# Another order of the same operations in a two-layer linear-attention and MLP kernel

## The chip, the cores and the metric

The kernel runs on one core of a Trainium2 chip. A time is the device time of one execution in microseconds (us); what counts is the median of several executions. The engines of a core run side by side and meet at semaphores: TensorE (PE in the profile, its weight loads PEld) multiplies matrices, VectorE (DVE), ScalarE (ACT) and GpSimd (POOL) work element by element, SyncE (SP) issues the DMA transfers. Each engine takes its instructions in the order in which the program gives them.

## The reference

Two layers of attention without softmax, each followed by an MLP with GELU, on `x` of 2048 rows and 448 columns. The same weights serve both layers.

```python
def _A_ref(x, wqkv, wo):
    ...
    phi = lambda t: jnp.where(t > 0, t + 1, jnp.exp(t)) + 1e-6
    pq, pk = phi(q), phi(k)
    kv = jnp.einsum("bhsd,bhse->bhde", pk, v)
    z = jnp.einsum("bhsd->bhd", pk)
    num = jnp.einsum("bhqd,bhde->bhqe", pq, kv)
    den = jnp.einsum("bhqd,bhd->bhq", pq, z)[..., None] + 1e-6
    o = num / den
    return (lambda x, *d: x.transpose(*d))(o, 0, 2, 1, 3).reshape(B, S, D) @ wo

def _B_ref(x, w1, b1, w2, b2):
    h = jnp.einsum("bsd,df->bsf", x, w1) + b1
    h = _gelu(h)
    return jnp.einsum("bsf,fd->bsd", h, w2) + b2

x = x + _A_ref(_layernorm(x, axis=-1), A_wqkv, A_wo)
x = x + _B_ref(_layernorm(x, axis=-1), B_w1, B_b1, B_w2, B_b2)
x = x + _A_ref(_layernorm(x, axis=-1), A_wqkv, A_wo)
x = x + _B_ref(_layernorm(x, axis=-1), B_w1, B_b1, B_w2, B_b2)
```

There are 16 heads of 28 columns; the MLP is 1792 wide.

## The kernel before, in words

**Number format.** A 32-bit operand goes through TensorE as a high and a low part (`hi`, `lo`), both in the format fp32r. A product of two such operands is made of three: hi by hi, hi by lo, lo by hi. ACT makes the high part by a copy, DVE or GpSimd the low part by a subtraction. The 448 columns are three pieces of 128 and a tail of 64; the tails of both parts share one piece, so a full product is 3 x 3 + 2 = 11 matmuls.

**Tiles.** The 2048 rows are 16 tiles of 128, and four blocks of four tiles. The MLP's 1792 inner columns are 14 chunks of 128; with four blocks this gives 56 chunks to a layer, counted through: chunk n belongs to block n // 14.

**Operations.** Each short function with `@op` gives one operation for a layer, a tile or chunk number and perhaps an engine. Those that matter here:

- Attention, first half, for each tile t: `ld` loads the rows, `a`, `ar`, `n` normalize them (statistics on DVE, a root on GpSimd, the norm on DVE). `T` turns the tile by four transposes on TensorE (with `d`, the tail's copy), or `tu` on DVE with `st` and `sp` through DRAM; `xh`, `xl` make its two parts. `K` and `Q` are products with the weights (lines 543 to 548), `ke`, `kp`, `kh`, `kl`, `za` and `qe`, `qp`, `qs` what follows on ACT, DVE and SP. `sh`, `sl` split the tile as it is, and `G` (lines 617 to 621) adds its product with K to four banks that stay for all 16 tiles.
- Attention, middle: `z`, `zb`, `dc`, `gt`, `kv`, `mask`, `m`, `mh`, `ml`, `mc` make the small matrices from G.
- Attention, second half, for each tile: `pl` loads the kept Q, `pz` (GpSimd), `pd`, `pm` (DVE) divide; `pT` (four transposes on TensorE) or `pu`, `ps`, `pp` turn it; `qh`, `ql` split it; `o` or `oc` are the products, `oa` adds to x; `la`, `ar`, `ln` normalize for the MLP, `mT` (TensorE) or `mu`, `ms`, `mp` turn, `yh`, `yl` split; `lb` adds the second bias on GpSimd.
- MLP, for each chunk: `f` is the first product, 11 matmuls of 512 columns (lines 850 to 854). `g` is the GELU on ACT (line 859), `gh` its high part on ACT, `gl` its low part on DVE (line 869). `y` is the second product, four groups `u` of three matmuls of 448 columns (lines 877 to 879), added up over the 14 chunks of a block in four banks. `ya` adds to x, `ys` stores.

**Buffers.** The PSUM banks are four for sums (`acc`), two for `f`, `Q` and `T` (`h`) and two others (`m`). The results of `g` have three buffers (ring `e`), and the rings `A` and `B` hold `gh` and `gl` of two chunks. A buffer is taken again when its last reader is done, which is a wait of the writer's engine.

**Order.** The whole schedule is written out by hand in `ORDER` (lines 15 to 110): two strings of tokens, one for each layer. `run` (lines 904 to 909) takes the tokens one by one and calls the operation; `>` in front of a token means the next layer, `<` the layer before, and an engine may follow a colon. So the text fixes the order of the instructions on each engine and on each DMA queue, and nothing else; the waits follow from which tile is written and read.

```python
    def run(l, text):
        for tok in text.split():
            up = (tok[0] == ">") - (tok[0] == "<")
            tok, _, e = tok.lstrip("<>").partition(":")
            name = tok.rstrip("0123456789")
            ops[name.replace("_", "")](l + up, int(tok[len(name):] or 0), e)
```

Of the kernel before, what the change touches and what calls it, by code (L numbers as in the profile page):

```python
# [16 lines left out]
        "ld0 a0 ar0 ld1 a1 n0 hot16 wkld0 wkld1:a wkld2 wkld3:a wkh1 wkl1 ht0 wkh0 ar1 wkl0 n1 d0 ht1 hx0 hl0 hk0 "  # L17
        "wkh2 wkl2 wkh3 d1 ht3 hx1 hl1 wqld0 wqh0 ht2 hx2 wkl3:p hk1 hx3 hl2 hk2 hl3 wql0 hk3 ld2 wqld1 wqh1 a2 "
        "ke0 kp0 bld1:xn wqld2 wqh2 wqld3 wqh3 kh0 sh0 wql2 wql3 wql1:p Q0 ar2 n2 d2 T2 sh1 sl0 kl0 G0 ld3 ld7 a3 "
        "za0 qe0 qp0 xh2 xl2 ke1 ld4 ld9 a4 kp1 kh1 ld6 bld0:xn sl1 ar4 n4 za1 ar3 ld5 n3 d3 a5 qs0 bhi0 ar5 blo0 "  # L20
        "Q1 qe1 K2 tab0 ke2 bld2:xn ld8 kl1 G1 T3 a7 qp1 n5 ar7 bhi1 blo1 kp2 a6 xh3 xl3 sh3 sh2 sl2 d4 kh2 Q2 T4 "
        "K3 n7 kl2 G2 ar6 qe2 bhi2 blo2 sl3 xh4 n6 za2 a8 qp2 tu6 tu7 ar8 bld3:xn ld10 qs1 bias1 xl4 a10 sh4 sl4 "
        "ar10 bld4:xn ke3 d5 bhi3 blo3 Q3 qs2 st3 ld11 ld12 bld5:xn kp3 n8 za3 n10 qe3 qp3 a11 kh3 bhi4 kl3 K4 "
        "ke4 kp4 Q4 kh4 T5 xh5 sp3 blo4 bhi5 blo5 ar11 fl kl4 qs3 xl5 tu10 n11 a9 za4 tu8 G3 G4 bld6:xn bld7:xn "
        "bias2 ld14 sh6 xh6 sl6 xl6 qe4 sh5 xh7 ar9 n9 ld13 tu9 st4 K5 bhi6 blo6 qp4 ke5 kp5 tu11 za5 sl5 bhi7 "
        "blo7 Q5 qe5 kh5 bld9:xn bhi9 qs4 a12 sp4 K6 ke6 qp5 qs5 xl7 kl5 kp6 kh6 za6 kl6 Q6 G5 K7 ar12 blo9 n12 "
        "bld8:xn st5 bld11:xn qe6 a14 xh8 bhi8 blo8 bld10:xn xh9 ke7 tu12 xl9 bhi11 sh7 a13 qp6 kp7 xl8 sp5 blo11 "
        "sl7 ar14 ar13 bhi10 kh7 kl7 n14 blo10 Q7 G6 qe7 sh8 qp7 K8 ld15 a15 n13 ke8 kp8 za7 G7 Q9 qs6 bld12:xn "
        "bhi12 sl8 blo12 ar15 qs7 bld13:xn tu14 kh8 tu13 xh10 sh9 za8 kl8 xl10 bhi13 blo13 K9 ke9 kp9 bld14:xn "
        "st6 bhi14 blo14 sl9 K10 ke10 kh9 Q8 qe8 bld15:xn bhi15 xh11 bld16:xn wo1 n15 kp10 za9 kl9 tu15 G8 G9 "  # L30
        "blo15 sh10 sl10 xl11 K11 sh11 sl11 kh10 kl10 bhi16 blo16 qp8 za10 G10 sp6 xh12 st7 xl12 K12 bld17:xn "
        "bld18:xn ke11 xh13 kp11 xl13 za11 qe9 kh11 bhi17 kl11 G11 ke12 kp12 za12 sh13 blo17 sl13 sh12 kh12 sl12 "
        "bhi18 sp7 xh15 K13 Q10 kl12 blo18 G12 xh14 xl14 K14 ke13 kp13 kh13 za13 kl13 xl15 K15 bld19:xn qs8 wo0 "
        "sh14 bld21:xn wv1 ld1 wv0 pl1 bhi19 qe10 blo19 ke14 bhi21 blo21 kp14 sl14 qp9 kh14 kl14 qp10 G13 G14 "
        "ke15 kp15 za14 za15 ld2 ld3 bld20:xn bld22:xn pl3 ld5 sh15 kh15 sl15 z zb pz1 kl15 G15 gt0 bhi20 Q11 dc "
        "pd1 gt3 gt1 gt2 kv pm1 pT1 Q12 pz3 pd3 pl2 pl0 blo20 pz0 mask pd0 m3 pm0 pz2 qs9 bld23:xn ld0 pd2 pm3 "
        "qh1 ql1 pT0 qh0 ql0 m0 mh0 ml0 m1 mh1 ml1 m2 mh2 ml2 mh3 ml3 pT3 qe11 pl4 pl7 bld24:W6 o0 pm2 ld6 pT2 "
        "oa0 qp11 qs11 qh2 bhi23 blo23 la0 o1 ql2 o2 oa1 ar0 ln0 lx0 mT0 bhi24 qh3 bhi22 la1 ql3 o3 oa2 yh0 ar1 "
        "blo22 la2 ln1 yl0 lx1 Q13 mT1 pz4 ar2 qe12 oa3 qp12 ln2 lx2 mT2 Q14 la3 ar3 yh1 yl1 ln3 qe13 qp13 lx3 "
        "bld25:W5 qs10 yh2 pd4 yl2 qe14 qp14 qs12 mT3 yh3 yl3 bhi25 blo25 pl5 pz5 Q15 qe15 qp15 qs14 qs15 qs13 "  # L40
        "blo24 f0 g0 gh0 pm4 lb1 pu4 pd5 pm5 gl0 f4 g4 f1 g1 gh1 u0 pl6 pz6 pd6 u3 u2 u1 f6 f2 g2 gl1 y1 bld27:W5 "
        "pu5 g6 gh2 gl2 f7 f3 g3 pm6 ps2 pp2 mc bld26:W6 pl8 pz7 pd7 gh3 y2 gl3 y3 f5 bhi26 qh5 gh4 pu6 ql5 oc5 "
        "pm7 gl4 ld4 y4 g5 qh4 gh5 bhi27 blo27 blo26 ql4 oc4 gl5 pu7 ps3 gh6 bld29:W5 ld7 bhi29 bld28:W6 ld8 pp3 "
        "pl9 f9 y5 g9 gh9 oa5 gl6 oa4 la4 y6 ar4 pz8 blo29 pd8 g7 qh6 qh7 f10 ln4 la5 gl9 mu4 ql7 ar5 pm8 ln5 gh7 "
        "gl7 mu5 g10 oc7 oa7 f11 g11 f8 g8 y7 f12 lb3 ql6 ms2 mp2 pl10 oc6 la7 ar7 gh8 gl8 y8 g12 ln7 oa6 la6 pz9 "
        "ar6 ln6 gh11 y9 lb2 bhi28 gh10 lb7 pd9 mu6 gl10 mu7 ms3 yh4 yh5 f13 mp3 pl11 y10 gh12 pm9 gl11 yl4 y11 "
        "g13 lb0 gl12 gh13 gl13 blo28 y12 yl5 y13 pz10 yh6 yh7 yl6 yl7 pu8 pd10 pu9 f14 g14 gh14 ya3 pm10 ya0 ya1 "
        "pl13 ys0 ys1 gl14 pu10 pz11 ya2 pd11 ps4 ys2 pp4 pl12 ys3 ld9 ld13 f15 g15 gh15 qh8 pm11 pu11 gl15 ql8 "
        "u58 u59 ld11 ps5 u56 f16 f17 u57 y15 g17 qh9 oc8 oa8 g16 pz12 tab1 gh16 gl16 f18 y16 la8 gh17 ql9 pd12 "
        "oc9 f20 pp5 pl15 qh10 g18 ql10 oc10 ar8 lb6 oa9 gl17 gh18 gl18 y17 ld10 g20 qh11 ln8 ql11 oc11 la9 lb8 "  # L50
        "ar9 pz13 ln9 gh20 oa11 pm12 mu8 f21 f19 la11 mu9 gl20 y18 g19 g21 pd13 f24 oa10 la10 pm13 gh19 gl19 y19 "
        "f22 y20 ar10 lb4 ar11 lb5 lb9 pl14 ln11 ln10 pz14 gh21 gl21 y21 lb11 g22 pd14 mu10 ms4 mp4 yh8 g24 gh22 "
        "gl22 gh24 yh9 mu11 pm14 ms5 f23 g23 y22 yl9 yl8 pu12 pu13 gh23 gl23 f27 g27 f25 mp5 yh10 yh11 yl11 g25 "
        "y23 yl10 pu14 gl24 f26 g26 gh25 gl25 f28 f30 y24 y25 gh26 gl26 y26 ps6 g28 g30 gh27 gl27 pz15 pd15 y27 "
        "ya7 ya5 ya4 >wkld0 pp6 ys7 ys5 gh28 gl28 f29 g29 qh13 u115 u112 u113 f34 pm15 ql13 pu15 gh29 gl29 oc13 "
        "oa13 ya6 f32 g32 u114 y29 qh12 gh30 gh32 la13 gl32 gl30 f31 g31 ps7 pp7 ld12 ld14 y30 g34 gh31 lb10 ql12 "
        "oc12 qh15 f35 oa12 gl31 y31 la12 ar12 ln12 lb12 mu12 ql15 qh14 ql14 g35 ar13 y32 f33 g33 gh33 >wqld0 "
        "oc14 oa14 gl33 ln13 la14 ar14 mu13 gh34 gl34 f37 f39 y33 ms6 ys6 ld15 mp6 >wqld1 ys4 >ld0 gh35 g37 >wkh1 "
        "g39 gl35 oc15 oa15 la15 ln14 mu14 ar15 ln15 mu15 ms7 lb15 y34 f38 f36 g36 gh36 y35 gh37 yh12 gl36 y36 "
        "gl37 y37 g38 gh38 gl38 y38 f40 gh39 gl39 mp7 yl12 yh15 yl15 >a0 yh14 yl14 lb13 f41 g41 yh13 yl13 g40 "  # L60
        "gh40 y39 f42 gh41 g42 gl40 y40 f43 f44 gh42 gl41 y41 g44 >wqh1 gh44 >wql1:p ya11 g43 ya8 ya9 >wkld1 ys8 "
        "ya10 gl42 f46 f45 g46 ys9 gl44 u169 u170 u168 u171 g45 gh43 gl43 ys10 >ld4 ys11 >ld2 >a2 >ar0 >n0 "
        ">wkl1:p f47 y43 y44 gh45 gl45 >wkh2 gh46 gl46 >wqh3 >wql3 y45 >ar2 >n2 >tu0 >ld1 >ld3 >a3 >a1 >ar1 >ar3 "
        "g47 gh47 >n1 >wqh2 f48 y46 >wkh3 g48 f50 >tu1 >a4 gl47 y47 gh48 >st0 g50 gh50 gl48 y48 f51 >wqh0 g51 "
        ">wql2 >ar4 >n4 gl50 f49 g49 f53 f52 gh49 gl49 y49 >wkl3 g52 gh51 >n3 >tu2 >wkl2 gl51 g53 f54 f55 y50 y51 "
        ">wkh0 gh52 gl52 y52 >wkl0 >tu3 >wql0 >sp0 >xh0 gh53 g55 g54 gl53 y53 gh54 >st1 gl54 y54 >sh0 >sl0 >xl0 "
        ">K0 gh55 gl55 y55 >tu4 >xh1 >xl1 ya13 ya12 >ld5 >sp1 lb14 ya14 ys13 ys12 >ld6 ya15 ys15 "
    ),
    (
        "ke0 Q0 K1 Q1 xh2 xh3 kp0 kh0 ke1 xl2 a5 ar5 xl3 n5 za0 tu5 qe0 <ys14 ld7 kl0 G0 a6 sh1 qe1 qp1 ld8 st2 "  # L70
        "sp2 sl1 kp1 kh1 kl1 a7 ar7 qp0 wo1 ld10 ar6 n6 za1 K2 ke2 kp2 kh2 kl2 za2 Q2 qe2 qp2 n7 tu6 ld9 qs1 qs2 "
        "xh4 sh3 xh5 xl4 a9 ar9 a8 n9 tu7 a10 ar8 Q3 G1 K3 ke3 n8 kp3 qe3 qp3 st3 sh2 sl3 sl2 kh3 Q4 K4 ke4 kl3 "
        "za3 xl5 kp4 G2 K5 G3 sh5 kh4 za4 ld12 ld11 ar10 sl5 tu8 tu9 n10 a12 tu10 kl4 sp3 qs0 xh6 xl6 Q5 ke5 sh4 "
        "qe4 kp5 kh5 a11 K6 ar12 sl4 G4 ke6 qp4 ar11 n11 tu11 xh7 st4 sp4 qs4 Q6 kl5 n12 xl7 kp6 qe5 qp5 sh6 sl6 "
        "kh6 ld13 a13 za5 qs3 st5 sp5 G5 K7 kl6 G6 ar13 tab0 sh7 qe6 xh8 tu12 n13 tu13 xl8 qp6 za6 ld14 qs5 ld15 "
        "a15 ke7 kp7 kh7 kl7 K8 ke8 Q7 a14 xh9 xl9 xh11 xl11 sh8 sl7 G7 ar15 za7 kp8 n15 qe7 qp7 kh8 sh9 K9 st6 "
        "sp6 xh12 kl8 ke9 kp9 za8 sl8 ar14 G8 n14 tu14 xh10 xl10 Q9 za9 sh10 sl10 xh13 kh9 kl9 tu15 st7 K10 ke10 "
# [863 lines left out]
```

## Time and profile before

| what | value |
|---|---|
| runs | 880.39 us median of three (880.34 to 881.69) |
| span of the profiled execution | 878.3 us |
| HBM read and written | 55.65 and 34.08 MB, 102 GB/s over the span |
| first attention stage, first MLP stage | about 20 to 140 us, 140 to 443 us |
| second attention stage, second MLP stage | about 443 to 575 us, 575 to 873 us |

The profile is a record of one execution. The span goes from its first to its last instruction; the run's time is some 2 us longer. "Busy" is the time in which an engine has an instruction in hand. Matmuls overlap on TensorE, so the duration of one (0.36 us for 448 columns) is longer than the distance between the starts of two (0.20 us), and it is the distance that adds up. In a timeline the columns are start, duration, engine, line, operation, written tile and read tiles, sizes, and how many were merged; in brackets the engine's idle time before it and what ended that. In a list of waits they are the waiting engine and line, what it waited for, then the total, the number and the longest in us.

### The profile page before, as it was taken

To read this page: it belongs to the slowest core of one execution; us is meant where nothing else is said; L and a number is where in the kernel's file an instruction comes from. 1 tells how busy PE (TensorE), PEld (TensorE's weight loads), DVE (VectorE), ACT (ScalarE), POOL (GpSimd) and SP (SyncE) were. 2 spreads that over 40 slices of the span, in tenths; PEclk is the share of its full clock that TensorE was granted. 3 is DMA by queue.
4 is the path that set the end of the run, shared out by engine and by line. 5 is a ranking of instruction groups with operands and counts; after the bars stand their busy time and mean duration, and the time that the engine had idled before them with its cause. 6 is when DMAs were issued, how large, how long until landed. Compare 5 with 4: busy or idle time off the path is not lost.

```text
span 878.3 us, 11548 instructions
## 1 busy us (share of the span) xinstructions
PE 873.2 (99%) x4181; PEld 772.4 (88%) x4181; DVE 473.7 (54%) x972; ACT 336.4 (38%) x596; POOL 202.6 (23%) x239
## 2 busy tenths in 40 slices
PE   9999999999999999999999999999999999999998
PEld 7999988889888888888899998988888888888887
DVE  7886587356574343324378765954572743343112
ACT  6777634332223221424355653333233132223221
POOL 4665543123132011010023333130220220130000
PEclk9999999999999999999999999999999999999999
DMA  6675732541613023221065452233125142120101
GB/s 210 175 234 171 222 95 98 159 130 58 213 58 117 30 82 103 78 84 49 24 206 160 138 182 85 94 124 99 65 88 166 46 119 84 39 96 5 38 1 43
DMA packets 62763, 93.71 MB, mean 107 GB/s; under 512 B 8817, under 2 KB 57969, under 8 KB 62705
## 3 DMA queue, kind: packets, MB, share of 16 engines
q1 hardware_dynamic: 62400, 92.51, 34.2%
q8 instruction: 33, 0.54, 0.3%
q10 hardware_dynamic: 304, 0.46, 0.2%
q14 instruction: 26, 0.20, 0.1%
HBM read 55.65 MB, written 34.08 MB: 102 GB/s over the span
## 4 chain that ended last, share of the span: by engine, by line
PE 99%; DVE 0%; ACT 0%; issue 0%; POOL 0%; POOLq 0%
PE y L878 10%; PE y L879 10%; PE y L877 10%; PE hp L851 9%; PE hp L852 9%; PE hp L850 9%; PE hp L854 3%; PE hp L853 3%; PE G L618 2%; PE psq L543 2%; PE G L617 2%; PE G L619 2%; PE psq L545 2%; PE psq L544 2%; PE psk L543 2%; PE psk L545 2%
## 5 line engine op out<-in xcount | busy, mean ns | idle before, releaser
L869 DVE TENSOR_TENSOR gl<-g,gh 128x512 fp32r<-128x512 f32 x112 | 79.8, 720 | 193.1 <-ACT gh L211 192.7
L878 PE MATMUL y<-w2l,gh 128*128 128x448 f32 x448 | 163.7, 365 | 0.0
L877 PE MATMUL y<-w2h,gh 128*128 128x448 f32 x448 | 163.6, 365 | 0.0
L879 PE MATMUL y<-w2h,gl 128*128 128x448 f32 x448 | 163.6, 365 | 0.0
L859 ACT ACTIVATE g<-hp,b1s 128x512 f32<-128x512 f32 x112 | 76.3, 688 | 227.8 <-PE hp L854 208.5
L851 PE MATMUL hp<-XH,w1l 128*128 128x512 f32 x336 | 131.2, 391 | 0.0
L852 PE MATMUL hp<-XL,w1h 128*128 128x512 f32 x336 | 131.1, 390 | 0.0
L850 PE MATMUL hp<-XH,w1h 128*128 128x512 f32 x336 | 131.1, 390 | 0.0
L211 ACT CAST gh<-g 128x512 fp32r<-128x512 f32 x112 | 69.1, 620 | 154.9 <-PE y L878 143.3
L357 POOL TENSOR_TENSOR brs<-bve,mhalf 128x1 f32<-128x1 f32 x64 | 41.0, 642 | 318.7 <-DVE bve L351 317.6
L877 PEld LDWEIGHTS y<-w2h,gh 128*128 128x128 f32 x448 | 84.1, 188 | 8.3
L878 PEld LDWEIGHTS y<-w2l,gh 128*128 128x128 f32 x448 | 84.1, 188 | 7.9
L879 PEld LDWEIGHTS y<-w2h,gl 128*128 128x128 f32 x448 | 84.1, 188 | 6.6
L852 PEld LDWEIGHTS hp<-XL,w1h 128*128 128x128 f32 x336 | 63.1, 188 | 13.6
L851 PEld LDWEIGHTS hp<-XH,w1l 128*128 128x128 f32 x336 | 63.1, 188 | 11.9
L850 PEld LDWEIGHTS hp<-XH,w1h 128*128 128x128 f32 x336 | 63.1, 188 | 11.8
L716 POOL TENSOR_TENSOR pz<-pq,zb 128x448 f32<-128x448 f32 x32 | 37.7, 1181 | 70.2 <-DVE dn L721 43.8
L535 POOL TENSOR_TENSOR xnl<-x,xnh 128x384 fp32r<-128x384 f32 x32 | 33.9, 1058 | 81.6 <-ACT xnh L211 81.2
L428 DVE TENSOR_TENSOR XL<-sp,XH 128x512 fp32r<-128x512 f32 x50 | 36.9, 752 | 22.7 <-ACT XH L211 22.5
L795 DVE TENSOR_TENSOR x<-op,x 128x448 f32<-128x448 f32 x32 | 19.8, 618 | 48.0 <-PE op L789 47.2
L853 PE MATMUL hp<-XH,w1x 128*128 128x512 f32 x112 | 43.6, 389 | 0.0
L854 PE MATMUL hp<-XL,w1x 128*128 128x512 f32 x112 | 43.6, 389 | 0.0
(162 smaller groups left out, 1573.1 us busy)
## 6 DMA issues: line engine op xcount, KB each, us to landing
x<-in_A_x_dram SPq DMA_DIRECT2D x32, 224.0 KB, 4.0
pq_d<-eq SPq DMA_DIRECT2D x32, 224.0 KB, 2.7
pq<-pq_d SPq DMA_DIRECT2D x32, 224.0 KB, 3.2
x<-x_d SPq DMA_DIRECT2D x32, 224.0 KB, 3.7
sq_a<-sq SPq DMA_DIRECT2D x13, 512.0 KB, 3.0
sp<-sq_a SPq DMA_DIRECT2D x52, 128.0 KB, 3.1
sq_q<-sq SPq DMA_DIRECT2D x12, 512.0 KB, 3.0
sp<-sq_q SPq DMA_DIRECT2D x48, 128.0 KB, 3.3
```

Source lines behind the costliest of these rows:

```text
L211: act.copy(out, src)
L357: pool.tensor_tensor(rs, ve, mhalf, op=OP.pow)
L850: pe.matmul(o, w1h[:, c, s], x.moving(x.hi, c), start=(c == 0), stop=False)
L851: pe.matmul(o, w1l[:, c, s], x.moving(x.hi, c), start=False, stop=False)
L852: pe.matmul(o, w1h[:, c, s], x.moving(x.lo, c), start=False, stop=False)
L853: pe.matmul(o, w1x[:, s], x.moving(x.hi, 3), start=False, stop=False)
L854: pe.matmul(o, w1x[:, s], x.moving(x.lo, 3), start=False, stop=True)
L859: act.activation(T[l, "g", n], T[l, "hp", n], AF.Gelu_apprx_tanh, bias=b1s[:, n % NF:n % NF + 1])
L869: dve.tensor_sub(lo, T[l, "g", n], f(hi))
L877: pe.matmul(o, gh[:, r], w2h[:, i, s], start=first, stop=False)
L878: pe.matmul(o, gh[:, r], w2l[:, i, s], start=False, stop=False)
L879: pe.matmul(o, gl[:, r], w2h[:, i, s], start=False, stop=last)
```

## The change

Only the text in `ORDER` is new; no operation, engine, buffer or tile size is. Both texts hold the same 2,122 operations, and the tokens that issue transfers (`ld`, `bld`, `qs`, `pl`, `st`, `sp`, `ps`, `pp`, `ms`, `mp`, `ys` and so on) come in the same sequence. The text is the same up to `d2`. Behind it, tokens have changed places: in the MLP the `f` of several chunks follow on each other and then the `y` of several; `T`, `pT` and `mT` of two tiles stand side by side; operations of ACT, DVE and GpSimd stand at other places between. The cut between the first and the second string has moved, too: operations that stood as `>wkl0` at the end of the first now stand at the start of the second, where `<gh51` is the first layer's.

```diff
-        "ke0 kp0 bld1:xn wqld2 wqh2 wqld3 wqh3 kh0 sh0 wql2 wql3 wql1:p Q0 ar2 n2 d2 T2 sh1 sl0 kl0 G0 ld3 ld7 a3 "
-        "za0 qe0 qp0 xh2 xl2 ke1 ld4 ld9 a4 kp1 kh1 ld6 bld0:xn sl1 ar4 n4 za1 ar3 ld5 n3 d3 a5 qs0 bhi0 ar5 blo0 "
-        "Q1 qe1 K2 tab0 ke2 bld2:xn ld8 kl1 G1 T3 a7 qp1 n5 ar7 bhi1 blo1 kp2 a6 xh3 xl3 sh3 sh2 sl2 d4 kh2 Q2 T4 "
...
+        "wqh1 a2 ke0 kp0 bld1:xn wqld2 wqh2 wqld3 wqh3 kh0 sh0 wql2 wql3 wql1:p Q0 ar2 n2 d2 ld3 ld7 ld4 ld9 "
+        "ld6 bld0:xn T2 za0 bhi1 qe0 kl0 sh1 sl0 G0 sl1 ke1 a3 qp0 ar3 a4 kp1 n3 xh2 ar4 xl2 n4 sh3 bhi0 blo0 "
+        "ld5 qs0 a5 bld2:xn ld8 Q1 qe1 a6 ar5 n5 qp1 kh1 K2 d3 za1 kl1 ke2 Q2 a7 T3 kp2 ar7 za2 xh3 kh2 xl3 ar6 "
+        "qe2 kl2 d5 d4 G1 K3 blo1 fl T4 n7 sh2 qp2 tu7 ke3 sl2 xh4 a8 T5 n6 ar8 kp3 G2 bld3:xn ld10 sl3 xl4 "
...
-        "yl1 la3 ar3 ln3 lx3 qe13 qp13 yh2 qs13 yl2 Q14 qe14 qp14 mT3 yh3 yl3 Q15 pd4 qe15 qs14 pl6 f0 g0 gh0 "
-        "qp15 qs15 gl0 pz5 pd5 pm5 pm4 pu4 f1 g1 gh1 pz6 pd6 lb2 lb3 pu5 pm6 gl1 u3 u0 u1 f2 g2 f4 g4 f5 u2 f3 g3 "
-        "y1 gh2 gl2 f6 y2 g5 ps2 mc pp2 qh4 gh3 pu6 ql4 gl3 f7 g7 gh5 qh5 lb1 pz7 pd7 ql5 oc4 f8 y3 pm7 pu7 ps3 "
...
+        "wkl0 <gh51 wqh2 <gl51 wqh0 <y50 ar3 n0 wkl1:p tu0 n3 a2 wql2 <y51 <f53 ar2 a1 ar1 n1 tu1 st0 sp0 <g53 "
+        "wqh3 <gh53 <f54 n2 <gl53 <g54 tu3 <f52 wql3 <f55 wkh3 <g52 <gh52 <gl52 xh0 <y52 <g55 xl0 <gh54 <gl54 "
+        "tu4 <y53 wkl2 xh1 wkl3 tu2 sh0 sl0 <y54 <gh55 K0 <gl55 wql1:p xl1 <y55 <ya13 ke0 K1 wql0 <ya12 <ya15 "
+        "kp0 <ya14 Q0 za0 kh0 st1 sh1 ld5 sp1 xh2 kl0 xh3 <ys13 <ys12 ld6 <ys15 <ys14 ld7 ld8 a5 ar5 qe0 n5 tu5 "
...
+        "f0 g0 gh0 pz6 f1 g1 f2 lb2 gh1 gl1 f3 gl0 u1 g3 u2 pd6 pz7 pd7 u0 u3 y1 pm7 g2 gh2 pm6 pu6 mc pu7 pp2 "
+        "ps3 pl9 pl8 pp3 gl2 y2 gh3 gl3 y3 tab1 f5 g5 f4 qh4 g4 gh4 pz9 f7 qh5 ql4 pd9 gl4 f6 g6 pz8 gh5 pd8 "
...
+        "gl16 oc10 y15 y16 pz15 oa8 pm13 la8 gh17 gl17 gh18 gl18 y17 y18 qh11 oc9 oa9 la9 f22 pd15 ar8 ln8 mu8 "
+        "oa10 g22 f20 f19 g20 gh20 ar9 ln9 lb9 pm15 la10 f21 gl20 ql11 g19 oc11 gh19 gl19 y19 y20 ar10 g21 gh21 "
+        "gh22 ln10 mu9 gl21 pm12 pu15 mu10 pu12 y21 gl22 y22 ms4 ys0 ld11 oa11 la11 f23 g23 f24 pu13 lb7 ar11 "
...
```

164 rows, old and new, of the table ORDER are left out of this document.

## The prediction

> **What bounds the kernel now.** I read the page first, then busy time by stretch, then the waits of the matrix engine alone, then single stretches of the timeline.
>
> ```profile
> span 878.3 us, 11548 instructions
> PE 873.2 (99%) x4181; PEld 772.4 (88%) x4181; DVE 473.7 (54%) x972; ACT 336.4 (38%) x596; POOL 202.6 (23%) x239
> ```
>
> ```profile
> 20.00:140.00 120.00, 120.00 (x615) 107.99 (x614) 94.49 (x197) 75.86 (x148) 61.91 (x75) 1.00 0.56 168
> 140.00:443.00 303.00, 303.00 (x1421) 266.48 (x1420) 141.00 (x284) 94.40 (x158) 54.11 (x54) 1.00 0.30 93
> 443.00:575.00 132.00, 131.97 (x668) 118.80 (x667) 98.06 (x209) 70.39 (x129) 37.17 (x51) 1.00 0.47 146
> 575.00:873.00 298.00, 298.00 (x1397) 262.10 (x1396) 123.75 (x245) 82.27 (x136) 40.21 (x38) 1.00 0.23 69
> ```
>
> ```profile
> PE hot L228 <- POOL ones L170: 1.1, 1, 1.1
> PE psk L489 <- ACT XH L211: 0.2, 1, 0.2
> PE tp L465 <- ACT tail L211: 0.2, 1, 0.2
> ```
>
> The columns of the stretches are PE, PEld, DVE, ACT and POOL. The column behind POOL is the granted clock, 1.00 throughout. From 20 to 873 us TensorE is as good as never seen idle, and its whole list of waits is 1.5 us long, all of it in the launch. So the time is the list of its 4,181 products at their spacing. A new order of the same products can win in three ways only: closer spacing, a shorter launch, a shorter end. The launch (up to the token d2) and the order of the last tokens (y54, y55, the ya and ys of the last four tiles) stay. That leaves the spacing. It can lose more: each product that now comes before its data adds its wait to the end one for one.
>
> **The change part by part.** Counted token by token, both orders hold the same 2,122 operations; the sequence of all tokens that issue a DMA is the same one, so each SP queue entry keeps its neighbours and only the time at which its data is ready can shift. No wait is added by hand; waits follow from the order.
>
> *First products in runs.* I took the TensorE tokens out of both texts. In the old order the 112 `f` stand in 72 runs (40 of one, 25 of two, 6 of three, 1 of four); in the new one in 25 (1 of two, 2 of three, 10 of four, 8 of five, 4 of six, so longer than the short description says). What a run's start costs is seen in the one run of four:
>
> ```profile
> 410.93 0.39 PE L850 MATMUL hp<-XH,w1h 128*128 128x512 f32 x1
> ...
> 413.45 0.39 PE L850 MATMUL hp<-XH,w1h 128*128 128x512 f32 x1
> ...
> 420.93 0.36 PE L877 MATMUL y<-w2h,gh 128*128 128x448 f32 x1
> ```
>
> ```profile
> 276.15 0.39 PE L850 MATMUL hp<-XH,w1h 128*128 128x512 f32 x1
> ...
> 278.66 0.39 PE L850 MATMUL hp<-XH,w1h 128*128 128x512 f32 x1
> ...
> 281.15 0.36 PE L877 MATMUL y<-w2h,gh 128*128 128x448 f32 x1
> ```
>
> The rows are starts of `f` operations (eleven products each). After a second product (`y`) the first takes 413.45 - 410.93 = 2.52 us, the three behind it (420.93 - 413.45) / 3 = 2.49 each; in the run of two, which also follows a `y`, 2.51 and 2.49. So a run costs 0.01 to 0.03 us to open, and I take 0.02. The new order opens 72 - 25 = 47 fewer: 47 x 0.02 = **0.94 us less**, with ends at 0.47 and 1.41. [...]
>
> *Transposes side by side.* Six more groups of four now follow directly on another group (T4 T5; pT1 pT3, mT1 mT0, mT2 mT3 in the first layer, where mT1 mT2 were adjacent before; pT2 pT3, mT0 mT1, mT3 mT2 in the second). One such pair and one single group are in the trace:
>
> ```profile
> 128.67 0.60 PE L390 MATMUL tp<-ident,xm 128*128 128x128 f32 x4
> 129.02 0.45 PE L774 MATMUL op<-Mh,qh 112*128 112x448 f32 x1
> 129.31 0.36 PE L775 MATMUL op<-Ml,qh 112*128 112x448 f32 x1
> ```
>
> ```profile
> 133.78 1.06 PE L390 MATMUL tp<-ident,xm 128*128 128x128 f32 x8
> 134.60 0.45 PE L543 MATMUL psq<-wq,XH 128*128 128x448 f32 x1
> 134.89 0.37 PE L544 MATMUL psq<-wq,XH 128*128 128x448 f32 x1
> ```
>
> Four transposes and the slow first product behind them take 129.31 - 128.67 = 0.64 us; a usual product of 448 columns is 0.20, so the group costs 0.44. Eight take 134.89 - 133.78 - 0.20 = 0.91, against twice 0.44 = 0.88. A pair is 0.03 dearer, not cheaper: 6 x 0.03 = **0.18 us more**. Its ends are nothing and 0.36, since the starts are rounded to 0.01. A gain I exclude: the first slow product is saved once per pair, and the 0.91 already contains that.
>
> *Spacing of the attention products.* The 448-column products of K, Q and G go at two paces, whatever their line:
>
> ```profile
> 60.78 0.37 PE L617 MATMUL G<-kh,xnh 128*128 128x448 f32 x1
> ...
> 62.84 0.37 PE L621 MATMUL G<-kl,xnh 128*128 128x448 f32 x1
> ```
>
> ```profile
> 94.74 0.37 PE L617 MATMUL G<-kh,xnh 128*128 128x448 f32 x1
> ...
> 96.77 0.37 PE L621 MATMUL G<-kl,xnh 128*128 128x448 f32 x1
> ```
>
> Each pair of rows is the first and the last of the eleven products of one G, ten gaps apart: 2.06 us, so 206 ns, and 2.03 us, so 203 ns. I found no operation that sets the pace. Some 600 products stand in the stretch from 20 to 140 us (615 by its row) and 668 in that from 443 to 575. If the flips fell so that 600 of these changed pace, it would be 600 x 3 ns = 1.8 us either way. I take **nothing**, and keep both ends.
>
> *Second products in runs.* This is where the order turns tight. `gh`/`gl` have two buffers each (rings A and B), so `gh` of a chunk waits until the `y` two places before it is done; then `gh` on ACT, `gl` on DVE, and the third product of the `y` needs `gl`. If the two `y` before stand right in front, all this must fit beside one `y`. In the old order 18 `y` are in that place, in the new one 53. The old one shows what room there is:
>
> ```profile
> 644.30 0.36 PE L879 MATMUL y<-w2h,gl 128*128 128x448 f32 x1
> 646.93 0.37 PE L877 MATMUL y<-w2h,gh 128*128 128x448 f32 x1
> 647.34 0.36 PE L879 MATMUL y<-w2h,gl 128*128 128x448 f32 x1
> ```
>
> ```profile
> 645.29 0.62 ACT L211 CAST gh<-g 128x512 fp32r<-128x512 f32 x1
> ```
>
> ```profile
> 645.78 0.65 DVE L428 TENSOR_TENSOR XL<-sp,XH 128x512 fp32r<-128x512 f32 x1
> 646.36 0.68 DVE L869 TENSOR_TENSOR gl<-g,gh 128x512 fp32r<-128x512 f32 x1
> ```
>
> The `y` two before ends at 644.30 + 0.36 = 644.66. With idle engines `gl` would be done 0.62 + 0.68 = 1.30 us later, at 645.96, and it is needed at 647.34: 1.38 us of room. Here ACT and DVE had other work in front, and `gl` ends at 647.04: 0.30 us of room, and TensorE did not wait. So a DVE operation of about 0.65 between two `gl` is free, two are just free, three are not, unless they ran earlier. I went through the new order's `y` runs with the longest DVE lists between two neighbouring `gl` and added durations from the rows. Most of those lists ran beside the `f` run in front (its four or more chunks give DVE 10 us and more). Two come out at the edge: in the second layer y2 (gl0, pd6, pd7, pm7, pm6, pu6, pu7 ahead of gl2, and pd7 behind GpSimd's pz7) with some 0.4 us of room, and y22 (pm12, pu15, mu10, pu12 ahead of gl22) with 0.1 to 0.3. I cost the 53 places at **0.1 us** in all; below nothing is impossible, as no wait is there to be removed, and the upper end is the second rival's 5.3 us.
>
> *Everything else.* Operations on ACT, DVE and GpSimd are only moved. TensorE covers them now from 20 to 873 us; where that cover fails the loss is a wait of TensorE, as above. In the attention stages K, Q and G come with less in between. The nearest place I worked out is the second layer's G0, which now stands behind K1 and Q0 alone: from the last `y`, DVE has ya13, wql0, ya12, ya15, kp0, ya14, za0 and kl0 to do, 8 x 0.58 (start to start, as XL and gl above) = 4.6 us, and K1, Q0 and G0's first product give 23 x 0.203 = 4.7. DVE is busy 94.5 of 120 us in the first attention stage, so it has little to give, and I put **0.3 us** on all these places, from nothing to 2 us (three or four misses of one DVE operation).
>
> The sum: -0.94 + 0.18 + 0 + 0.1 + 0.3 = **-0.4 us**. The profiled execution spans 878.3 us; the runs' median of 880.39 has 2.1 us around it, which the change does not touch. 880.39 - 0.4 = **880.0 us**.
>
> **The rivals.** *One: late low parts, slower.* GpSimd delays DVE:
>
> ```profile
> 705.94 1.15 POOL L716 TENSOR_TENSOR pz<-pq,zb 128x448 f32<-128x448 f32 x1
> 706.01 1.62 DVE L869 TENSOR_TENSOR gl<-g,gh 128x512 fp32r<-128x512 f32 x1 [1.04 <-ACT gh L211]
> ```
>
> A `gl` that started 0.07 us behind a `pz` took 1.62 us in place of 0.68: 0.94 more. [...] A plain place with 1.38 us of room survives one such hit, but not one hit plus one DVE operation (0.94 + 0.65 = 1.59). GpSimd is busy 54.1 of 303 us in the first MLP stretch, some 18%, so about 53 x 0.18 = 10 of the 53 places meet it; half of them with another DVE operation in front, at 0.2 to 0.9 each, and the same in attention, makes 2.5 to 5.3 us over the -0.76 of the first two terms: **882.1 to 885**. For it: the room seen fell to 0.30 us with 18 such places, and now there are 53. Against it: where GpSimd's and DVE's operations meet is fixed by the order, and the old order let no `y` wait. [...]
>
> *Two: the pace falls well, faster.* All attention at 203 ns and no new wait: 880.39 - 0.76 - 0.9 to 1.8 (half or all of the 600 products at 206 ns now; the quoted rows show both paces in use) = **877.8 to 878.7**. No row says that the new order drives it there.
>
> [...]
>
> *Four: the slow pace spreads* to the other half of attention: 880.0 + 1.8 = **881.8**.
>
> **How the numbers follow.** Forecast (879.4 to 880.7) 0.5; rival one 0.2; two 0.12; three 0.1; four 0.08. 0.2% of 880.39 is 1.76 us, about what a measurement of this kernel tells from no change: faster means under 878.63, slower over 882.15. Rival two lies nearly all below the first bound, with a little from a forecast whose terms all fall well: 0.13 faster. Rival one lies above the second, with a little of four: 0.21 slower. 0.66 same. The range goes from 878.3 to 883.0: it holds all of the forecast, three and four, half of rival two and the lower part of rival one, so some 0.2 are left out.
>
> **What would show it.** In the profile after, an `f` behind a `y` still takes 2.51 to 2.52 us and there are 25 of them; every other `f` takes 2.49. Busy TensorE and the span fall together by under 1.5 us. Pairs of transposes take 0.91 us. TensorE's list of waits stays at a few rows; if rows such as y or G waiting for DVE's gl or kl appear, with over 2 us together, rival one holds and I was wrong on the room. If the gap of K, Q and G is 203 ns throughout, rival two holds. I am wrong altogether if the span moves by over 2 us with no wait of TensorE and no change of pace.

## The result, and the profile after

The changed kernel takes 890.26 us (median of five runs, 887.75 to 891.92) against 880.34 us for the kernel before (five runs, 879.67 to 881.69): a ratio of 1.0109, with a 95% interval of 1.0094 to 1.0125. It is slower by some 10 us where 880.0 was forecast, and it lies above the whole range. In what follows the lines of the changed kernel are those of the kernel before plus 3 (`f` at L853, `y` at L880 to L882).

The page after, its span and its busy times:

```profile
span 889.2 us, 11538 instructions
PE 877.1 (99%) x4181; PEld 776.3 (87%) x4181; DVE 473.3 (53%) x972; ACT 337.3 (38%) x596; POOL 199.5 (22%) x239
```

The span is 889.2 - 878.3 = 10.9 us longer with the same 4,181 products; DVE, ACT and GpSimd are as busy as before within 3.1 us. Busy time by stretch (PE, PEld, DVE, ACT, POOL, then the granted clock), the stretches set by the stages of this kernel:

```profile
20.00:145.00 125.00, 122.26 (x615) 109.38 (x615) 93.63 (x198) 73.98 (x145) 63.12 (x75) 0.99 0.55 163
145.00:449.00 304.00, 304.00 (x1428) 267.84 (x1427) 143.95 (x284) 96.89 (x161) 50.86 (x52) 1.00 0.30 92
449.00:586.00 137.00, 133.22 (x663) 120.56 (x662) 100.96 (x215) 69.46 (x128) 38.69 (x53) 0.98 0.46 141
586.00:884.00 298.00, 297.53 (x1397) 261.88 (x1396) 118.67 (x241) 83.07 (x135) 37.18 (x37) 1.00 0.22 69
```

Both attention stages have lost TensorE time, 125.00 - 122.26 = 2.7 and 137.00 - 133.22 = 3.8 us, and in both the granted clock is below 1.00; before, it was 1.00 there and at most 0.03 us was idle. The MLP stages, where the many new runs of `f` and `y` stand, lost 0.5 us in all. The waits of TensorE name the two attention stages too:

```profile
PE G L620 <- ACT kh L579: 5.1, 2, 3.1
PE G L621 <- DVE kl L583: 1.4, 2, 0.7
PE hot L231 <- POOL ones L173: 1.1, 1, 1.1
PE y L882 <- DVE gl L872: 0.5, 1, 0.5
```

The 5.1 us are two waits of G for `kh`, one in each layer, and the 1.4 us the two for `kl` that follow at once. In the timeline of TensorE the first place is this:

```profile
97.18 0.37 PE L551 MATMUL psk<-wk,XL 128*128 128x448 f32 x1
99.55 0.47 PE L620 MATMUL G<-kh,xnh 128*128 128x448 f32 x1 [2.01 <-ACT kh L579]
100.75 0.47 PE L621 MATMUL G<-kl,xnh 128*128 128x448 f32 x1 [0.72 <-DVE kl L583]
...
101.96 0.57 PE L620 MATMUL G<-kh,xnh 128*128 128x448 f32 x1
102.33 0.57 PE L621 MATMUL G<-kl,xnh 128*128 128x448 f32 x1
...
105.25 0.37 PE L547 MATMUL psk<-wk,XH 128*128 128x448 f32 x1
```

and the second:

```profile
463.02 0.37 PE L551 MATMUL psk<-wk,XL 128*128 128x448 f32 x1
466.45 0.47 PE L620 MATMUL G<-kh,xnh 128*128 128x448 f32 x1 [3.06 <-ACT kh L579]
467.64 0.74 PE L621 MATMUL G<-kl,xnh 128*128 128x448 f32 x1 [0.72 <-DVE kl L583]
468.18 0.57 PE L622 MATMUL G<-kh,xnl 128*128 128x448 f32 x1
...
473.78 0.38 PE L546 MATMUL psk<-wk,XH 128*128 128x448 f32 x1
```

Read the starts. From 97.18 to 105.25 us there are 16 gaps between neighbouring products; at the usual 0.203 they would take 3.25 us, they take 8.07: **4.8 us lost**. From 463.02 to 473.78 there are 18; they take 10.76 instead of 3.65: **7.1 us lost**. Together with 0.7 us at the `y` in the list (start to start too; its wait alone is 0.5) that is 12.6 us; the rest of the kernel is 12.6 - 10.9 = 1.7 us faster than before. In each place the loss has two parts: the waits for `kh` and `kl`, and behind them a stretch in which every gap is 0.37 us (102.33 - 101.96) in place of 0.20: eight gaps in the first place, fifteen from 468.18 on in the second, 23 x 0.17 = 3.9 us. The granted clock is exactly one half there, by the busy time of that stretch (columns as above):

```profile
101.90:105.00 3.10, 3.10 (x10) 2.71 (x10) 1.16 (x2) 0.45 (x1) 1.93 (x3) 0.50 0.00 0
```

**What was late in the first layer.** ACT's timeline in the changed kernel, and for its DMA issues of L316 (the loads `bld` of the weights) between 60 and 110 us the time from issue to landing and who waited:

```profile
97.42 0.56 ACT L214 CAST w2h<-stg 128x448 fp32r<-128x448 f32 x1 [3.17 <-DMA stg<-in_B_w_dram]
...
98.88 0.62 ACT L579 ACTIVATE kh<-psk,tiny 128x448 fp32r<-128x448 f32 x1
```

```profile
  ACT w2h L214: 3.2, 1
...
DMA to landing us min/median/max: 2.5/2.9/6.5
```

The first row is `bhi21`, a cast of an MLP weight that is not needed for a long time. In the new order it stands right behind K14 and ahead of xh15, sh13 and kh13 (the row at 98.88). Its load needed 6.5 us, against a median of 2.9, and ACT stood still for 3.17 us at the head of its list. In the old order `bhi21` stood behind `blo19` and `ke14`, and did not wait; there the same load was issued at 93.65 us and landed after 2.5 us.

**What was late in the second layer.** Of the changed kernel: the timeline of SP's queue, a row of what it waited for, and the timelines of GpSimd and of DVE:

```profile
456.90 0.32 SPq L438 DMA_DIRECT2D x<-x_d  x1
...
458.26 0.93 SPq L438 DMA_DIRECT2D x<-x_d  x2
```

```profile
SPq L438 <- POOL xnh L539: 3.2, 1, 3.2
```

```profile
454.92 0.55 POOL L360 TENSOR_TENSOR brs<-bve,mhalf 128x1 f32<-128x1 f32 x1 [9.26 <-DVE bve L354]
...
456.40 0.47 POOL L539 TENSOR_TENSOR xnh<-x,xnh 128x64 fp32r<-128x64 f32 x1
```

```profile
463.21 0.63 DVE L350 BATCH_NORM_STATS2 bst<-x 128x6 f32<-128x448 f32 x1 [4.00 <-DMA x<-x_d]
...
465.10 0.62 DVE L561 SCALAR_TENSOR_TENSOR psk<-psk,ek 128x448 f32<-128x448 f32 x1
```

From the bottom: DVE's `a7` waited 4.00 us for its load, with `kp1` (465.10) behind it, and so `kh1` and G1 came late. The load `ld7` was issued at 458.26 because `ld6`, ahead of it on SP, went out at 456.90 only: it waited for GpSimd's `sl1` (L539, done at 456.87), and that stood behind `ar5`, for which GpSimd had been idle for 9.26 us. In the kernel before, `ld6` was issued at 446.82. Both kernels issue the same entries on SP in the same sequence, but not into the same buffers. In the compiled program before, `ld6` writes the buffer that tile 13 of the layer before leaves with its store; in the changed one it writes the buffer of tile 1, which is free when `sl1` has read it. The tiles take their buffers in the order in which the text frees them, and the new text frees others first.

### The profile page after: what moved, and what is told of

Same layout as the page of the kernel before. It is cut to its first block, busy times and chain, and to the rows that moved or that the text cites. A ratio compares the mean times of both kernels' runs of the same rounds, so it can differ in the third digit from the quotient of the medians.

```text
span 889.2 us, 11538 instructions
## 1 busy us (share of the span) xinstructions
PE 877.1 (99%) x4181; PEld 776.3 (87%) x4181; DVE 473.3 (53%) x972; ACT 337.3 (38%) x596; POOL 199.5 (22%) x239
## 4 chain that ended last, share of the span: by engine, by line
PE 96%; DVE 2%; DMA 1%; ACT 1%; issue 0%; POOL 0%; SPq 0%; POOLq 0%; DVEq 0%; ACTq 0%
PE y L882 10%; PE y L880 10%; PE y L881 10%; PE hp L854 9%; PE hp L853 9%; PE hp L855 9%; PE hp L857 3%; PE hp L856 3%; PE G L621 2%; PE G L622 2%; PE G L620 2%; PE psq L546 2%; PE psq L547 2%; PE psq L548 2%; PE psk L546 2%; PE psk L548 2%
## 5 line engine op out<-in xcount | busy, mean ns | idle before, releaser
L872 DVE TENSOR_TENSOR gl<-g,gh 128x512 fp32r<-128x512 f32 x112 | 82.2, 738 | 247.1 <-ACT gh L214 246.9
L882 PE MATMUL y<-w2h,gl 128*128 128x448 f32 x448 | 163.7, 365 | 0.5 <-DVE gl L872 0.5
L880 PE MATMUL y<-w2h,gh 128*128 128x448 f32 x448 | 163.6, 365 | 0.0
L853 PE MATMUL hp<-XH,w1h 128*128 128x512 f32 x336 | 130.8, 389 | 0.0
L360 POOL TENSOR_TENSOR brs<-bve,mhalf 128x1 f32<-128x1 f32 x64 | 38.4, 602 | 363.6 <-DVE bve L354 353.2
L882 PEld LDWEIGHTS y<-w2h,gl 128*128 128x128 f32 x448 | 84.1, 188 | 7.5 <-DVE gl L872 0.8
L880 PEld LDWEIGHTS y<-w2h,gh 128*128 128x128 f32 x448 | 84.1, 188 | 7.1
L853 PEld LDWEIGHTS hp<-XH,w1h 128*128 128x128 f32 x336 | 63.1, 188 | 12.6
L854 PEld LDWEIGHTS hp<-XH,w1l 128*128 128x128 f32 x336 | 63.1, 188 | 12.6
L350 DVE BATCH_NORM_STATS2 bst<-x 128x6 f32<-128x448 f32 x64 | 39.7, 620 | 13.6 <-DMA x<-x_d 8.0
```

The source lines that it names most:

```text
L350: dve.bn_stats(st, xs)
L853: pe.matmul(o, w1h[:, c, s], x.moving(x.hi, c), start=(c == 0), stop=False)
L854: pe.matmul(o, w1l[:, c, s], x.moving(x.hi, c), start=False, stop=False)
L872: dve.tensor_sub(lo, T[l, "g", n], f(hi))
L880: pe.matmul(o, gh[:, r], w2h[:, i, s], start=first, stop=False)
L882: pe.matmul(o, gl[:, r], w2h[:, i, s], start=False, stop=last)
```

## The experiments

The theory after this reading: the loss lies in the attention's order alone, at two places where an operation that waits for a transfer stands at the head of an engine's list, and the half clock behind each wait is the wait's consequence. The rivals: that the new runs of the MLP cost something (the prediction's first rival), and that no single place is to blame but an order that is dense everywhere.

**Half of the change at a time.** Two kernels (`att_old_mlp_new` and `att_new_mlp_old`) take the attention stages from one text and the MLP stages from the other. The first begins, against the changed kernel, with

```diff
-        "wqh1 a2 ke0 kp0 bld1:xn wqld2 wqh2 wqld3 wqh3 kh0 sh0 wql2 wql3 wql1:p Q0 ar2 n2 d2 ld3 ld7 ld4 ld9 "
+        "a2 ke0 kp0 bld1:xn wqld2 wqh2 wqld3 wqh3 kh0 sh0 wql2 wql3 wql1:p Q0 ar2 n2 d2 T2 sh1 sl0 kl0 G0 ld3 "
...
```

and its last chunks of layer 1 (from f42 on) are in the old order, so that it has 29 runs of `f` and not 25.

> Attention in the old order, MLP in the new one (29 runs of first products). Late landings in attention are the whole loss: 878.5 to 879.6 us, by about 43 runs x 0.02 us faster than before, and no wait of TensorE over 0.3 us. Rival, low parts late in the long runs of second products: 884 us or more, with waits of y for gl.

Measured: 879.5 us (ten runs) against 880.58, ratio 0.9986 (0.9976 to 0.9996). The second is the opposite.

> Attention in the new order, MLP in the old one (70 runs of first products). Late landings in attention: 889 to 892 us, with the two waits of G near 97 and 463 us and the clock at half behind them. Rival, low parts late in the runs of second products: within 1 us of before, 880 to 881.5 us.

Measured: 890.1 us, ratio 1.0111 (1.0092 to 1.0129), with the same waits of G, 4.5 us for `kh` in two (5.1 in the changed kernel), in TensorE's list (its lines lie 7 further on):

```profile
PE G L627 <- ACT kh L586: 4.5, 2, 2.8
```

So the whole loss is the attention's order, and the MLP's order by itself is a gain of 880.58 - 879.5 = 1.1 us, by the interval 0.4 to 2.1.

**One entry moved in each layer.** `bhi21` behind `kh14` in layer 1 (`late_bhi21`):

```diff
-        "xl14 wv1 ke13 K14 bhi21 kp13 xh15 sh13 sl13 kh13 blo19 xl15 sh14 sl14 ld1 za13 kl13 G13 K15 ke14 kp14 "
-        "kh14 kl14 G14 ke15 Q10 wv0 pl1 ld2 sh15 ld3 blo21 za14 kp15 kh15 za15 kl15 z zb dc qe10 sl15 G15 gt3 "
+        "xl14 wv1 ke13 K14 kp13 xh15 sh13 sl13 kh13 blo19 xl15 sh14 sl14 ld1 za13 kl13 G13 K15 ke14 kp14 "
+        "kh14 kl14 bhi21 G14 ke15 Q10 wv0 pl1 ld2 sh15 ld3 blo21 za14 kp15 kh15 za15 kl15 z zb dc qe10 sl15 G15 gt3 "
```

> New order, but ACT takes bhi21, which waits for a transfer, behind kh14 in place of before sh13 and kh13. The landing is the cause of the first wait: 884.5 to 886 us (890.3 less the 5.2 us over the usual spacing between 80 and 120 us). Rival, the stage is simply too dense and the wait only moves to the next G: 888.5 us or more.

Measured: 887.21 us (885.52 to 887.39), ratio 1.007 (1.0055 to 1.0085): 3.0 us better than the changed kernel, less than was expected. From 95 to 106 us TensorE is busy throughout again, at full clock, as the busy time of this stretch shows:

```profile
95.00:106.00 11.00, 11.00 (x57) 10.18 (x56) 5.43 (x10) 5.84 (x11) 6.18 (x8) 1.00 0.75 210
```

The place is mended. Why only 3.0 us came of the 4.8 I read there is not settled. K has a wait of 0.9 us for `xl` that is absent from the changed kernel's list of waits. And the profiled execution took 885.52 us, inside the expected range, with a mean granted clock of 0.997; the other three took 1.6 to 1.9 us longer, at 0.995 to 0.996. That fits another stretch at half clock in them: one of 3.4 us, as the profiled execution has in layer 2 (its granted clock from 455 to 475 us is 0.91), costs 1.7. In layer 2, `a7` and `a6` behind `kl1` (`late_a7`):

```diff
-        "sl1 xl2 G0 qp0 xl3 a7 Q1 a6 ke1 kp1 kh1 za1 kl1 Q2 ar6 K2 G1 K3 qe1 qp1 ar7 n6 Q3 sh2 sl2 n7 ke2 kp2 "
+        "sl1 xl2 G0 qp0 xl3 Q1 ke1 kp1 kh1 za1 kl1 a7 Q2 a6 ar6 K2 G1 K3 qe1 qp1 ar7 n6 Q3 sh2 sl2 n7 ke2 kp2 "
```

> New order, but in the second layer DVE takes a7 and a6, which wait for loaded rows, behind kl1 in place of before kp1. The landing is the cause of the second wait: 882.5 to 884 us (890.3 less the 7.1 us over the usual spacing between 460 and 480 us). Rival, the stage is too dense and the wait moves on to K3, Q3 or G2: 887 us or more.

Measured: 890.07 us, no gain. G1 started on time, and the wait went to K4; the waits of TensorE and DVE's timeline:

```profile
PE psk L546 <- DVE kl L583: 4.3, 1, 4.3
```

```profile
471.89 0.63 DVE L350 BATCH_NORM_STATS2 bst<-x 128x6 f32<-128x448 f32 x1 [2.24 <-DMA x<-x_d]
...
473.37 0.61 DVE L583 SCALAR_TENSOR_TENSOR kl<-psk,kh 128x448 fp32r<-128x448 f32 x1
```

Now `a9` stands at the head of DVE's list for its own late load, with `kl2` behind it. So the place of one load's reader is not the whole cause: SP is late from `ld6` on, and with it the loads behind.

**The buffer of `ld6`.** This kernel (`ld6_other_buffer`) moves `sh1` and `sl1`, and by that the buffer that `ld6` gets, and nothing on SP:

```diff
-        "kp0 <ya14 Q0 za0 kh0 st1 sh1 ld5 sp1 xh2 kl0 xh3 <ys13 <ys12 ld6 <ys15 <ys14 ld7 ld8 a5 ar5 qe0 n5 tu5 "
-        "sl1 xl2 G0 qp0 xl3 a7 Q1 a6 ke1 kp1 kh1 za1 kl1 Q2 ar6 K2 G1 K3 qe1 qp1 ar7 n6 Q3 sh2 sl2 n7 ke2 kp2 "
+        "kp0 <ya14 Q0 za0 kh0 st1 ld5 sp1 xh2 kl0 xh3 <ys13 <ys12 ld6 <ys15 <ys14 ld7 ld8 a5 ar5 qe0 n5 tu5 "
+        "xl2 G0 sh1 sl1 qp0 xl3 a7 Q1 a6 ke1 kp1 kh1 za1 kl1 Q2 ar6 K2 G1 K3 qe1 qp1 ar7 n6 Q3 sh2 sl2 n7 ke2 kp2 "
```

> The changed kernel with two entries of layer 2's attention moved: sh1 from before ld5 and sl1 from before xl2 to behind G0. By the compiled programs the load of block 6 then takes the buffer that the store ys13 frees, as it did in the kernel before, and no longer the one that GpSimd's sl1 frees. First theory (layer 2's stall comes from ld6 waiting in SP's FIFO for GpSimd's sl1, 456.9 us, with ld7 behind it): ld6 issues some 4 us earlier, a7 and kp1 on VectorE no longer wait for it, G1 starts on time, and of the 7 us lost at 460 to 480 us 4 to 7 go: 883 to 886. Rival (the loads come late anyway, since SP's queue is late as a whole at this place, as with a7 moved): the wait moves on to another load, and the time stays at 888 or above. The stall of layer 1 stays in both.

Measured: 883.35 us (882.22 to 888.53), ratio 1.0045 (1.0024 to 1.0066): 6.9 us less than the changed kernel. SP's timeline in this kernel (`ld6`, then `ld7` and `ld8`):

```profile
449.19 0.32 SPq L438 DMA_DIRECT2D x<-x_d  x1
...
450.56 3.96 SPq L438 DMA_DIRECT2D x<-x_d  x2
```

`ld6` goes out 456.90 - 449.19 = 7.7 us earlier, and the 3 us wait of G1 is gone. What is left of layer 2's stall is 1.0 us of K4 behind `a9`, at full clock (1.00 from 455 to 475 us). Not all of the 6.9 us is layer 2's, though. `bhi21` stands where it stood, but in the profiled execution it waited 2.01 us for its load in place of 3.17, and the first place lost 2.1 us in place of 4.8, at full clock (1.00 from 95 to 106 us). Layer 2's part is seen better between two kernels that both have `bhi21` out of the way: `three_mended` below takes 887.21 - 880.69 = 6.5 us less than `late_bhi21` (with `yl6` moved as well).

**Is the half clock the wait's own?** In `hot_in_the_gap`, fifteen products of ones, with no use made of the result, fill TensorE's gap ahead of G13; they read constants, and G13 and all behind it begin no earlier than before:

```diff
-        "xl14 wv1 ke13 K14 bhi21 kp13 xh15 sh13 sl13 kh13 blo19 xl15 sh14 sl14 ld1 za13 kl13 G13 K15 ke14 kp14 "
+        "xl14 wv1 ke13 K14 bhi21 kp13 xh15 sh13 sl13 kh13 blo19 xl15 sh14 sl14 ld1 za13 kl13 hot15:h G13 K15 ke14 kp14 "
```

> The changed kernel with 15 products of ones (512 columns, 0.227 us each, 3.4 us, results unused) ahead of layer 1's G13, where TensorE otherwise stands idle from 97.4 to 99.6 and from 99.8 to 100.8 us. Theory (the clock halves because TensorE stood idle): the stretch of 12 products at 373 ns from 102 to 105 us is gone, though G13 and all behind it begin no earlier: 2 us less than the changed kernel, 888. Rival (the halved clock comes from something else that happens there, or from the dense stretch before): the stretch at 373 ns stays, and the time is that of the changed kernel, 890. Layer 2's stall stays in both.

Measured: 888.14 us (887.15 to 888.59), 2.1 less than the changed kernel for 15 products more. `kh13` is as late as before (98.74 us against 98.88), and the products behind run at 0.20 us (ACT's and TensorE's timelines in this kernel):

```profile
98.74 0.62 ACT L579 ACTIVATE kh<-psk,tiny 128x448 fp32r<-128x448 f32 x1
```

```profile
97.50 3.61 PE L231 MATMUL hot<-ones 128*128 128x512 f32 x15
100.95 0.36 PE L620 MATMUL G<-kh,xnh 128*128 128x448 f32 x1
101.15 0.37 PE L621 MATMUL G<-kl,xnh 128*128 128x448 f32 x1
```

So in layer 1 the half clock is a second price of standing idle. The rows show it; the 2.1 us alone would not, since in this profile layer 2 was at half clock for a shorter time as well, though nothing there was changed and its waits of G are as long (3.10 and 0.72 us against 3.06 and 0.72). The busy time of the same stretch in the changed kernel, then in this one:

```profile
455.00:475.00 20.00, 16.22 (x64) 14.01 (x63) 14.49 (x31) 7.96 (x16) 4.92 (x8) 0.83 0.57 171
```

```profile
455.00:475.00 20.00, 16.18 (x71) 14.15 (x70) 14.91 (x34) 8.01 (x16) 3.92 (x8) 0.91 0.63 191
```

In layer 2 it was not tried in this way, since no PSUM bank is free there.

**All the places mended.** `three_mended` has the buffer of `ld6` and `bhi21` as above, and `yl6` behind `y11` in layer 2's MLP, for the 0.5 us of `gl`:

```diff
-        "gl10 g11 gh11 yl4 y10 yh7 pm10 yl6 gl11 g13 y11 gh12 yh5 gh13 gl12 gl13 y12 y13 yl5 pu10 lb1 yl7 f15 "
+        "gl10 g11 gh11 yl4 y10 yh7 pm10 gl11 g13 y11 yl6 gh12 yh5 gh13 gl12 gl13 y12 y13 yl5 pu10 lb1 yl7 f15 "
```

> The same two moves, with the cast bhi21 behind kl14 (layer 1) and yl6 behind y11 (layer 2's MLP, so that gl11 comes out 0.5 us earlier). If these three places hold all that the new order lost, what is left is its gains of spacing, 2 to 2.5 us below the kernel before: 878 to 880. If the order is late in more places than these three, or each mended place lets another wait appear: 882 to 886.

Measured: 880.69 us, ratio 1.001 (0.9996 to 1.0024), with ten runs from 878.52 to 883.8, a wider spread than the 879.29 to 881.42 of the kernel before beside it. That is between the two outcomes expected. What moving `yl6` gives is not shown: the wait of `y` for `gl` is absent, too, from the lists of `late_bhi21`, `ld6_other_buffer` and `hot_in_the_gap`, where `yl6` stands as in the changed kernel. The profiled execution still had `a9` waiting 1.15 us for its load and K4 1.0 us behind it. So `a9` was moved as well (`four_mended`):

```diff
-        "za2 tu7 tu6 qe2 st2 sp2 wo1 ld10 ld9 qs1 a9 xh4 qp2 kh2 kl2 xl4 K4 a10 sh3 xh5 ar9 ke3 kp3 kh3 tab0 "
+        "za2 tu7 tu6 qe2 st2 sp2 wo1 ld10 ld9 qs1 xh4 qp2 kh2 kl2 xl4 a9 K4 a10 sh3 xh5 ar9 ke3 kp3 kh3 tab0 "
```

> The kernel of three_mended with layer 2's a9 behind xl4 on VectorE, so that the load that it waits for (1.15 us in three_mended's profile, with kl2 behind it and K4 on TensorE 1.0 us late) holds up nothing that TensorE waits for. If that wait is what is left of the loss: 878 to 880, and a narrower scatter of the executions than 878.5 to 883.8. If other loads, near their due time, cost most executions something at other places: 880 to 882, the scatter as wide as before.

Measured: 878.45 us (877.52 to 879.37) against 880.18, ratio 0.9976 (0.9966 to 0.9987). This is 1.7 us under the kernel before, and the interval leaves out 1. Its list of waits is about as short as that of the kernel before:

```profile
PE hot L231 <- POOL ones L173: 1.1, 1, 1.1
PE psk L548 <- DVE XL L431: 0.8, 1, 0.8
PE tp L468 <- ACT tail L214: 0.4, 2, 0.2
```

The last kernel (`five_mended`) moves `a7` and `a6` behind `kl1` in that one too, as in the diff further up.

> The kernel of four_mended with a7 and a6 behind kl1 too, so that no statistics of these three blocks stand ahead of a kp, kl or za that is due. If the scatter of three_mended comes from a7's load, which lands near its due time there: 878 to 879.5 and executions within 1.5 us of each other. If it comes from another place: as four_mended.

Measured: 878.4 us (877.17 to 880.56), ratio 0.9976 (0.9967 to 0.9985): no better, and its runs lie 3.4 us apart, not 1.5. So the upper half of three_mended's spread went with `a9`, and moving `a7` and `a6` too shows no further gain.

## Why the prediction was wrong, point by point

- **What bounds the kernel.** Right on the list of TensorE's products, wrong on "one for one": waits of 2.01 + 0.72 and 3.06 + 0.72 us were followed by a stretch at half clock, which cost 3.9 us more here.
- **First products in runs, 0.94 us less.** Right in mechanism and nearly in size, with some luck. In TensorE's timeline of the changed kernel (fence below) an `f` behind a `y` takes 164.58 - 162.06 = 2.52 us and the next 167.07 - 164.58 = 2.49 (starts of L853). The 25 runs are there, as counted, but not every one opens slowly: the first `f` takes 2.51 us or more in 20 of 25, as it did in 68 of 72 before, and 2.49 in the others. What all 112 `f` take beyond 2.493 us each adds up to 1.50 us before and 0.42 after: 1.08 less. So behind another product the eleven mostly take a little longer here.

```profile
162.06 0.39 PE L853 MATMUL hp<-XH,w1h 128*128 128x512 f32 x1
...
164.58 0.39 PE L853 MATMUL hp<-XH,w1h 128*128 128x512 f32 x1
...
167.07 0.39 PE L853 MATMUL hp<-XH,w1h 128*128 128x512 f32 x1
```

- **Transposes side by side, 0.18 us more.** Mis-sized, within its ends. A pair takes 137.31 - 136.23 - 0.20 = 0.88 us, twice a single group's 0.44, so it costs nothing (TensorE's timeline of the changed kernel):

```profile
136.23 1.04 PE L393 MATMUL tp<-ident,xm 128*128 128x128 f32 x8
...
137.31 0.37 PE L547 MATMUL psq<-wq,XH 128*128 128x448 f32 x1
```

- **Pace of the attention products, nothing, with 1.8 us on either side.** Within its ends. Gaps of 205 to 214 ns between two products of K, Q and G number 527 in the profiled execution before, 374 after, 226 in four_mended; at 4 ns each the last is (527 - 226) x 4 = 1.2 us. What sets the pace stays open: with the attention in the old order and only the MLP new there were 440, and among the kernels with the attention in the new order the number goes from 226 to 615 (att_new_mlp_old). So these 1.2 us can't be put down to the order.
- **Second products in runs, 0.1 us; rival one, late low parts.** Nearly right (the upper end of 5.3 us, which the prediction gives to the second rival, is that of rival one). Of the 53 tight places one failed, at neither of the two I had named: `y11` of layer 2 waited 0.5 us for `gl11`. Rival one had the right sign, less than half of the size, and the wrong mechanism: the waits are for ACT's `kh` and DVE's `kl`, each behind a transfer, and not for a `gl` that ran beside a `pz`.
- **Everything else, 0.3 us, from nothing to 2.** This is the step that failed, by some 12 us. The prediction put it so: "the sequence of all tokens that issue a DMA is the same one, so each SP queue entry keeps its neighbours and only the time at which its data is ready can shift". The sequence did stay. But the tile that each load writes depends on which buffers the text has freed by then, and so what a load waits for can change with no token on its queue moved; `ld6` went from a store to `sl1`. So the text of `ORDER` does not fix the sequences "and nothing else", as the description of the kernel before puts it; it hands out the buffers, too. And the same step set moved ACT and DVE operations against TensorE's products alone, never against the landing of the loads that they read. The two operations `bhi21` and `a7` need no more time than before; they stand earlier than their data, and all that is behind them on their engine stands there with them. Their loads landed later after their issue, too: 6.5 us in place of 2.5 for `bhi21`, and 4.9 in place of 3.5 at most for `a7`.

- **Rivals two to four.** Two (the pace) came in part in the profiled execution, 527 - 374 slow gaps fewer, and its gain was covered by the stalls; three (nothing gained by the runs) does not fit the 1.1 us that the MLP's order gives by itself, nor the second products, whose starts show no loss in `four_mended` against the kernel before; four (a slower pace) did not come in the changed kernel.

The terms that were worked out from rows gave -0.94 + 0.18 + 0 + 0.1 = -0.66. With the stalls mended, the median is 880.18 - 878.45 = 1.7 us under the kernel before, and the profiled execution's span 878.3 - 875.8 = 2.5, of which 1.1 are the `f` and 1.2 the pace of that execution. That the 11 us more came from two stalls of attention is shown by the runs that mend them; that the load of `bhi21` was slow because of its neighbours (DMA engines 80% busy from 88 to 98 us, with a transfer of 392 KB issued 0.7 us ahead; in the kernel before 3.6 us ahead, with the DMA engines 71% busy) is argued only.

## What to carry to other kernels

When an order written by hand is changed, the queue's sequence being the same doesn't mean that its times are: look up which buffer each load gets in the old and in the new program, and which operation frees it. Put an operation that waits for a transfer behind those of its engine that TensorE needs next, since the landing of the loads of L316 varied from 2.5 to 6.5 us here, and what stood at the head of a list held up all of it (ACT for 3.17 us at `bhi21`, DVE for 4.00 us at `a7`). And waits of TensorE can cost more than their length: here 2.01 + 0.72 = 2.7 us of listed waits cost 4.8, and 3.06 + 0.72 = 3.8 cost 7.1.

## What the runs showed of the hardware

The clock halved behind waits of a few microseconds, and with a delay. In the changed kernel waits of 2.01 and 0.72 us, one product apart, were followed by 3.4 us at half clock (0.50, from 101.75 to 105.16), which began 4.2 us after TensorE first stood idle. Waits of 3.06 and 0.72 us were followed by 6.8 us (466.97 to 473.80), begun 3.6 us after. The length of the wait does not settle how long the half clock lasts: waits of 3.10 and 0.72 us in hot_in_the_gap were followed by 3.4 us only (466.40 to 469.82; the granted clock from 455 to 475 us is 0.91 there, 0.83 in the changed kernel). In att_new_mlp_old the shorter of the two pairs was of 4.5 - 2.8 = 1.7 and 0.7 us; the mean granted clock of that execution, 0.996, does not tell behind which pair it halved. Waits of 0.87 and 0.71 us in ld6_other_buffer (TensorE's timeline), at the place of the 2.01 and 0.72, were followed by no half clock (1.00 from 95 to 106 us):

```profile
97.44 0.47 PE L620 MATMUL G<-kh,xnh 128*128 128x448 f32 x1 [0.87 <-ACT kh L579]
98.62 0.47 PE L621 MATMUL G<-kl,xnh 128*128 128x448 f32 x1 [0.71 <-DVE kl L583]
```

So 2.01 + 0.72 = 2.73 us of waits had a stretch at half clock behind them, and 0.87 + 0.71 = 1.58 us had none; what lies between is not shown.
